# Four late pairs scored with queries on partitions and weights transposed by DMA, in clustered attention followed by a gated MLP, with a listed order of operations

## The chip, the cores and the metric

The kernel runs on one core of a Trainium2 chip. The metric is the device time of one launch in microseconds (us). Five engines work side by side, each with its own instruction queue in program order: TensorE (PE in the profile, PEld its weight loads), VectorE (DVE), ScalarE (ACT), GpSimd (POOL) and SyncE (SP). SP here does nothing but issue DMAs. PSUM holds what TensorE writes; SBUF holds everything else.

## The reference

```python
# q, k, v: (4, 8, 768, 64); centroids: (8, 16, 64)
q_assign = argmax(q_n . c_n)            # nearest of 16 centroids, per head
k_assign = argmax(k_n . c_n)
scores = where(q_assign == k_assign, q @ k.T / sqrt(64), -1e9)
scores = scores - max(scores, -1)
attn = exp(scores); attn = attn / (sum(attn, -1) + 1e-9)
x = (attn @ v), heads side by side      # (4, 768, 512)

h = maximum(x @ w_in, 0)                # w_in (512, 1024)
u, v = h[..., :512], h[..., 512:]
v_n = (v - mean(v)) / sqrt(var(v) + 1e-6)
v_s = w_spatial @ v_n + b_spatial       # over the 768 positions
out = (u * v_s) @ w_out                 # (4, 768, 512)
```

A query with no key in its cluster gets equal weights on all keys, since every score is -1e9 before the maximum is taken off.

## The kernel before

**Work.** There are 4 batches of 8 heads; the kernel takes the heads in 16 pairs, numbered 0 to 15, four to a batch. 768 positions are NT = 6 blocks of P = 128. To keep precision, each operand is split into a high and a low f16 part (`hq` and `lo` for keys and queries, `vhl` for values, `pt[:, 0]` and `pt[:, 1]` for the weights), and products are summed in PSUM.

**`prep(n)`** loads keys and queries of a pair, transposed (`raw`), and values (`vraw`), splits them, and works out the cluster of each key and query as one-hot rows. Those rows, scaled by PEN, stand below the 64 rows of the head in `hq`, so that a matmul over 80 rows adds a bonus where clusters agree. The low parts are made by `low`, on POOL for the entries of `POOL_LOWS` (a scaling and a subtraction, L531 and L532), and in one VectorE operation elsewhere (L533). `values` makes the parts of V and also the sums of V over all positions (for pairs 8 to 15 by a VectorE reduction `vs`, L684, and two small matmuls, L685), which go by two small DMAs into `mean`.

**`shifts(n)`** works out the largest score of every query ahead of attention. For each head it scores queries against keys with the high parts alone, with queries on partitions (L728: 6 matmuls of 512 columns and 6 of 256), reduces each group over the keys on VectorE (L735, nine per head, into `nm`), and turns the result into three columns on ScalarE (L752, L755). A DMA transpose (`sht`, L761) and a small copy (L762) put them as rows into `hq`.

**`attend(n)`** goes over the six key blocks k of each head with keys on partitions. `scores` does 4 matmuls into a PSUM buffer `sc` (L782, L784; the row of L784 takes the query's maximum off). ScalarE does the exponential into `p32` (L788) and rounds it into `pt[:, 0]` (L790), POOL makes `pt[:, 1]` (L791). With keys on partitions `pt` is already what the next matmul needs, and `values` (L796) adds 18 small matmuls into `av`. For k = 0 it also adds six matmuls of `hq` with `mean`, which serve the queries with no key in their cluster. The sum of weights is a 65th column. At the end of a head the result is divided, split again (L815 to L820) and, for the pair, transposed by one DMA into `xT` (L822).

**`mlp(b)`** runs the dense layers of batch b on TensorE in groups of matmuls of 512 columns (L840: `win` with `xT`, `wsp` with `vn`, `wou` with `gT`), which are put between the attention of the batch behind it. The product `u * v_s` is split on VectorE and POOL (L901 to L903) and transposed by DMA (`gT`, L904).

**Order.** Every operation is an object with an engine, a cost, what it comes after and the buffers that it takes. `Plan.run` goes through a modelled time with these costs, and at each step takes from what is ready on the engine that is free first the operation with the lowest due time plus key:

```python
k = o.key if o.key >= FILLER else (g if o.due is None else o.due) + o.key
if pick is None or (k, o.seq) < pick[:2]:
    pick = (k, o.seq, o)
```

The engines' queues follow this order. Buffers go round in rings: `r_sc` has 2 PSUM buffers of 768 columns in use, `r_acc` 4 of 512, `r_p32` 3, `r_pt` 4, `raw` and `vraw` 1 each, `hq` and `lo` 4. All DMAs but the stores of results stand on SP's queue in this order.

```python
r_sc = R(None, "sc", None, None, 2, free_order=True, tiles=[...])
r_acc = R(None, "acc", None, None, 4, free_order=True, tiles=[...])
```

## Time and profile before

| | |
|---|---|
| median of 3 runs (lowest to highest) | 680.63 us (679.72 to 682.48) |
| the profiled execution: time, span | 677.58 us, 675.8 us |
| TensorE busy, mean granted clock | 629.0 us, 0.995 |
| VectorE, ScalarE, POOL busy | 467.3, 433.5, 440.9 us |
| data moved by DMA | 70.49 MB, 104 GB/s |

Busy time is the time in which at least one instruction of the engine runs; matmuls overlap, so the busy times of groups of matmuls add up to more than TensorE's. A granted clock of 1.00 is TensorE's full speed. "Idle before, releaser" in a row is the time in which the engine stood still in front of the instruction and what it waited for. SPq is SP's queue of DMA issues: a row of it shows how long the issue held the queue, not when the data land. The pairs follow one another; the first four fill the time to about 150 us, then the dense layers of the batch behind run beside the next four, and from 592 us on only the dense layers of batch 3 are left.

### The profile page before, as it was taken

What the parts mean: (1) busy time and instruction counts of PE and PEld (TensorE: products, weight loads), DVE (VectorE), ACT (ScalarE), POOL (GpSimd) and SP (SyncE); (2) the same over time, 40 slices, a digit from 0 to 9 for tenths busy, and PEclk for the clock granted to TensorE, in tenths of its full rate; (3) what the DMA queues carried; (4) which work ended last, traced back from release to release, by engine and by line L of the source; (5) the groups of instructions that cost most, each with busy time, mean ns of one, the idle gap of its engine ahead of it and who ended that gap; (6) DMA issues with size and microseconds to landing.
All of it is one profiled execution on the core that took longest, in us unless ns stands there. A gap on an engine that the chain in (4) does not pass through costs nothing.

```text
span 675.8 us, 16854 instructions
## 1 busy us (share of the span) xinstructions
PE 629.0 (93%) x6821; PEld 378.0 (56%) x6821; DVE 467.3 (69%) x939; ACT 433.5 (64%) x685; POOL 440.9 (65%) x312
## 2 busy tenths in 40 slices
PE   2877898999999999999999999999999999989996
PEld 2455565766556655566465655566555655634442
DVE  5889999999899989285898857285795720215210
ACT  3586998998788946297586748387594837422011
POOL 6764798998786965376678747567486856703210
PEclk9988999999999999999999999999999999999999
DMA  5666667567728374374615346263300213130123
GB/s 171 177 166 126 169 171 169 94 166 175 175 66 207 64 138 127 84 167 111 147 26 130 60 91 139 45 144 84 80 14 14 52 29 82 38 85 1 31 63 93
DMA packets 106029, 70.49 MB, mean 104 GB/s; under 512 B 89640, under 2 KB 92768, under 8 KB 105952
## 3 DMA queue, kind: packets, MB, share of 16 engines
q1 hardware_dynamic: 102352, 63.13, 41.5%
q10 hardware_dynamic: 3600, 6.30, 2.5%
q8 instruction: 53, 0.87, 0.5%
q14 instruction: 24, 0.20, 0.1%
HBM read 27.63 MB, written 6.29 MB: 50 GB/s over the span
## 4 chain that ended last, share of the span: by engine, by line
PE 60%; DVE 17%; DMA 7%; ACT 7%; POOL 4%; issue 3%; SPq 1%; ACTq 0%; POOLq 0%; DVEq 0%
PE acc L840 35%; PE acc L796 9%; DVE nm L735 8%; PE sc L782 5%; PE sc L784 5%; PE acc L728 4%; ACT p L788 3%; ACT pt L790 2%; DMA vraw<-in_vp_dram 2%; DMA oht<-ohx 1%; DMA gT<-ghl 1%; POOL pt L791 1%; SPq L662 1%; POOL raw L531 1%; DVE vs L684 1%
## 5 line engine op out<-in xcount | busy, mean ns | idle before, releaser
L791 POOL TENSOR_TENSOR pt<-p,pt 128x768 f16<-128x768 f32 x192 | 322.5, 1698 | 83.8 <-ACT pt L790 44.6
L788 ACT ACTIVATE p<-sc,plog 128x768 f32<-128x768 f32 x192 | 169.2, 898 | 46.6 <-PE sc L784 43.5
L735 DVE TENSOR_REDUCE nm<-acc 128x1 f32<-128x512 f32 (+1 forms) x288 | 180.5, 678 | 13.0 <-PE acc L728 12.7
L790 ACT CAST pt<-p 128x768 f16<-128x768 f32 x192 | 155.6, 830 | 14.7 <-PE acc L796 12.9
L796 PEld LDWEIGHTS <-pt 128*128 128x128 f16 x3456 | 124.8, 98 | 22.8 <-POOL pt L791 4.0
L796 PE MATMUL acc<-vhl,pt 128*128 128x65 f16 (+1 forms) x3456 | 133.0, 194 | 3.0 <-POOL pt L791 2.8
L840 PE MATMUL acc<-win,xT 128*128 128x512 f16 x576 | 129.8, 379 | 0.0
L728 PE MATMUL acc<-hq 80*128 80x256 f16 (+1 forms) x384 | 95.6, 335 | 9.1 <-DVE nm L735 3.9
L782 PE MATMUL sc<-hq,lo 128*128 128x512 f16 (+1 forms) x384 | 94.8, 328 | 5.1 <-ACT p L788 4.7
L840 PE MATMUL acc<-vn,wsp 128*128 128x512 f16 x432 | 97.0, 379 | 0.8 <-DVE nm L735 0.8
L784 PE MATMUL sc<-hq 81*128 81x512 f16 (+1 forms) x384 | 94.9, 328 | 0.0
L840 PEld LDWEIGHTS <-xT 128*128 128x128 f16 x576 | 55.1, 98 | 62.5
L901 DVE SCALAR_TENSOR_TENSOR u<-acc,bsp,u 128x512 f32<-128x512 f32 x24 | 17.9, 746 | 90.9 <-PE acc L840 90.9
L903 POOL TENSOR_TENSOR ghl<-u,ghl 128x512 f16<-128x512 f32 x24 | 27.8, 1158 | 69.1 <-DVE ghl L902 65.2
L840 PEld LDWEIGHTS <-wsp 128*128 128x128 f16 x432 | 41.7, 98 | 49.6 <-issue 1.3
L840 PE MATMUL acc<-wou,gT 128*128 128x512 f16 x288 | 65.6, 379 | 3.8 <-DMA gT<-ghl 3.8
L911 ACT ACTIVATE o<-acc 128x512 f32<-128x512 f32 x24 | 14.3, 596 | 62.0 <-PE acc L840 43.3
L728 PEld LDWEIGHTS <-hq 80*128 80x128 f16 x384 | 34.2, 99 | 32.3 <-issue 12.5
L784 PEld LDWEIGHTS <-hq 81*128 81x128 f16 x384 | 37.6, 98 | 26.1 <-issue 1.0
L782 PEld LDWEIGHTS <-lo 128*128 128x128 f16 x384 | 34.2, 98 | 30.3 <-issue 14.4
L840 PEld LDWEIGHTS <-gT 128*128 128x128 f16 x288 | 27.4, 98 | 35.6 <-DMA gT<-ghl 4.8
L882 POOL TENSOR_TENSOR vn<-v,vn 128x512 f16<-128x512 f32 x24 | 30.0, 1268 | 17.3 <-DVE vn L881 17.3
(124 smaller groups left out, 652.1 us busy)
## 6 DMA issues: line engine op xcount, KB each, us to landing
raw<-in_kqT_dram SPq DMA_DIRECT2D x15, 768.0 KB
vraw<-in_vp_dram SPq DMA_DIRECT2D x16, 384.0 KB
out_dram<-o ACTq DMA_DIRECT2D x24, 256.0 KB
hq<-hq SPq DMA_DIRECT2D x15, 384.0 KB
vn<-in_w_in_dram SPq DMA_DIRECT2D x8, 512.0 KB
hq<-lo SPq DMA_DIRECT2D x15, 192.0 KB
lo<-hq SPq DMA_DIRECT2D x15, 192.0 KB
wraw<-in_wsT_dram SPq DMA_DIRECT2D x12, 192.0 KB
```

Source lines behind the costliest of these rows:

```text
L728: T.matmul(out=acc.t[:, c:c + cs.stop - cs.start], lhsT=hq.t[0:R_SH, 1, h, t * P:(t + 1) * P], rhs=hq.t[0:R_SH, 0, h, cs], start=c == 0, s ...
L735: V.tensor_reduce(out=nm.t[:, t, k:k + 1] if n == 1 else nm.t[:, t:t + n, k], in_=src, axis=AX.X, op=ALU.max, negate=True)
L782: T.matmul(out=sc.t[:, cs], lhsT=lo.t[:, h, ks], rhs=hq.t[:, 2, h, cs], start=True, stop=False)
L784: T.matmul(out=sc.t[:, cs], lhsT=hq.t[0:R_E, 0, h, ks], rhs=hq.t[0:R_E, 1, h, cs], start=False, stop=True)
L788: o = op("ACT", 0.9, lambda sc=sc, p32=p32: A.activation(out=p32.t, in_=sc.t[:, 0:S], func=AF.Exp, bias=plog, scale=SC_UNIT), after=[o, m_ ...
L790: o = op("ACT", 0.83, lambda pt=pt, p32=p32: A.copy(out=pt.t[:, 0, :], in_=p32.t), after=[o], use=[p32], new=[pt], key=K_HI)
L791: o = op("POOL", 1.65, lambda pt=pt, p32=p32: G_.tensor_tensor(out=pt.t[:, 1, :], in0=p32.t, in1=pt.t[:, 0, :], op=ALU.subtract), after=[o ...
L796: T.matmul(out=av.t[:, t * (D + 1):t * (D + 1) + w], lhsT=lhsT, rhs=rhs, skip_group_check=True, **f)
L840: T.matmul(out=acc.t, lhsT=lr[m][0], rhs=lr[m][1], start=(m == 0), stop=(m == n - 1))
L882: l = op("POOL", 1.25, lambda t=t, v=v: G_.tensor_tensor(out=vn[:, 1, t, :], in0=v.t, in1=vn[:, 0, t, :], op=ALU.subtract), after=[h], use ...
L901: o = op("DVE", 0.75, lambda: V.scalar_tensor_tensor(out=u32.t, in0=acc.t, scalar=bsp[:, t:t + 1], in1=u32.t, op0=ALU.add, op1=ALU.mult), ...
L903: l = op("POOL", 1.156, lambda: G_.tensor_tensor(out=ghl.t[:, 1, :], in0=u32.t, in1=ghl.t[:, 0, :], op=ALU.subtract), after=[h], use=[u32, ...
```

## The change

Three things change in what is computed, and the order of all operations with them.

1. Pairs 9, 11, 13 and 15 (`ROWS`) have no `shifts` and no `mean`. They are attended by a new function, `attend_rows`, which goes over the six query blocks t with queries on partitions. The scores are the same four matmuls with the operands exchanged. VectorE finds each query's maximum from the scores themselves (one reduction over 768 keys and two operations on one column), and the exponential takes it as bias and a scale, which is 0 where no key is in the cluster. The weights now have queries on partitions, so a DMA transpose on SP (`ptT`, two buffers) turns the 128x1536 high and low weights of a block before 18 value matmuls.
2. `low` on POOL gives its scaling to ScalarE, and head 1 of pair 0 is no longer in `POOL_LOWS`.
3. The planner is gone. `Plan.run` takes the operations from a list of numbers, `ORDER`. A buffer taken "in order of freeing" is now the one whose last user has the earliest place in the list. The units of work become half pairs (`Unit`); `SPLIT` is False, so that the halves are the heads as before. In the function for results, the scale `f` is a name of its own. `vs` lies in a buffer for weights.

```diff
-POOL_LOWS = {(0, 1), (0, 2), (1, 0), (1, 1), (1, 2)}
+PTT_BUFS = 2
+ROWS = (9, 11, 13, 15)
+POOL_LOWS = {(0, 2), (1, 0), (1, 1), (1, 2)}
...
     def run(self):
...
+        for turn, i in enumerate(ORDER):
+            o = self.ops[i]
+            assert all(a.turn < turn for a in o.after)
+            for tok in o.new:
+                tok.ring.taken.append(tok)
+                tok.alloc()
+            o.turn = turn
+            if o.fn is not None:
+                o.fn()
+
+ORDER = [
+    0, 10, 7, 9, 1, 12, 2, 11, 3, 13, 4, 162, 14, 15, 16, 17, 18, 19, 20, 21, 163, 22, 6, 23,
...
         if (n, x) in POOL_LOWS:
-            o = op("POOL", 1.0, lambda: G_.tensor_scalar(out=raw(), in0=raw(), scalar1=scale, scalar2=None, op0=ALU.mult), after=after, use=use, key=key)
+            o = op("ACT", lambda: A.activation(out=raw(), in_=raw(), func=AF.Copy, scale=scale), after=after, use=use)
...
     def values(...):
...
+        if n in ROWS:
+            X["v"] = [o_vh, o_vl]
+            return
...
     def shifts(...):
+        if u.n in ROWS:
+            return
...
+    def attend_rows(u):
+        n, h = u.n, u.part
+        X = pair[n]
+        hq, lo, vh = X["hq"], X["lo"], X["vhl"]
+        av = r_acc.new()
+        prev = None
+        for t in range(NT):
+            sc, p32, pt, ptT, nq = r_sc.new(), r_p32.new(), r_pt.new(), r_ptT.new(), r_nq.new()
+            ts = slice(t * P, (t + 1) * P)
+
+            def scores(sc=sc, ts=ts):
+                for cs in halves:
+                    T.matmul(out=sc.t[:, cs], lhsT=hq.t[:, 2, h, ts], rhs=lo.t[:, h, cs], start=True, stop=False)
+                for cs in halves:
+                    T.matmul(out=sc.t[:, cs], lhsT=hq.t[0:R_SH, 1, h, ts], rhs=hq.t[0:R_SH, 0, h, cs], start=False, stop=True)
+
+            o = last["sc"] = op("PE", scores, after=X["go"][h] + [last.get("sc")] + exps[-2:-1], use=[hq, lo], new=[sc])
+            o = op("DVE", lambda sc=sc, nq=nq: V.tensor_reduce(out=nq.t[:, 0:1], in_=sc.t[:, 0:S], axis=AX.X, op=ALU.max, negate=True), after=[o], use=[sc], new=[nq])
+            o = op("DVE", lambda nq=nq: V.tensor_scalar(out=nq.t[:, 1:2], in0=nq.t[:, 0:1], scalar1=LIM, scalar2=SC_UNIT, op0=ALU.is_lt, op1=ALU.mult), after=[o], use=[nq])
+            o = op("DVE", lambda nq=nq: V.tensor_scalar(out=nq.t[:, 2:3], in0=nq.t[:, 0:1], scalar1=nq.t[:, 1:2], scalar2=P_LOG * LN2, op0=ALU.mult, op1=ALU.add), after=[o], use=[nq])
+            o = op("ACT", lambda sc=sc, p32=p32, nq=nq: A.activation(out=p32.t, in_=sc.t[:, 0:S], func=AF.Exp, bias=nq.t[:, 2:3], scale=nq.t[:, 1:2]), after=[o], use=[sc, nq], new=[p32])
+            exps.append(o)
+            o = op("ACT", lambda pt=pt, p32=p32: A.copy(out=pt.t[:, 0, :], in_=p32.t), after=[o], use=[p32], new=[pt])
+            o = op("POOL", lambda pt=pt, p32=p32: G_.tensor_tensor(out=pt.t[:, 1, :], in0=p32.t, in1=pt.t[:, 0, :], op=ALU.subtract), after=[o], use=[p32, pt])
+            o = sp(lambda pt=pt, ptT=ptT: nc.sync.dma_start_transpose(ptT.t, pt.t.rearrange("p a s -> p (a s)")), after=[o], use=[pt], new=[ptT])
+
+            def values(ptT=ptT, t=t):
+                def mm(w, lhsT, rhs, **f):
+                    T.matmul(out=av.t[:, t * (D + 1):t * (D + 1) + w], lhsT=lhsT, rhs=rhs, skip_group_check=True, **f)
+
+                for k in range(NT):
+                    mm(D + 1, ptT.t[:, k], vh.t[:, k, h, 0:D + 1], start=t == 0 and k == 0, stop=False)
+                    mm(D, ptT.t[:, k], vh.t[:, k, h, D + 2:], start=False, stop=False)
+                    mm(D + 1, ptT.t[:, NT + k], vh.t[:, k, h, 0:D + 1], start=False, stop=t == NT - 1 and k == NT - 1)
+
+            prev = op("PE", values, after=[o, prev] + X["v"], use=[ptT, vh] + ([av] if t else []), new=[] if t else [av])
+        results(u, av, prev)
```

How the list moves instructions is shown at three places. The first is POOL at the start of the program. Before, behind the last constants, it makes the low parts of head 1 of pair 0, of its values (`vhl_89`), of both heads of pair 1 and of its values (`vhl_90`):

```order
L531 TENSOR_SCALAR raw<-raw 128x768
L532 TENSOR_TENSOR lo<-raw,hq 128x768
L531 TENSOR_SCALAR vraw<-vraw 128x768
L532 TENSOR_TENSOR vhl_89<-vraw,vhl_89 128x12x64
L531 TENSOR_SCALAR raw<-raw 128x768
L532 TENSOR_TENSOR lo<-raw,hq 128x768
```

After, there is no scaling, the values of pair 0 come first, and a constant stands behind the lows; then the first pass over weights (`pt`) follows:

```order
L523 TENSOR_TENSOR vhl_89<-vraw,vhl_89 128x12x64
L523 TENSOR_TENSOR lo<-raw,hq 128x768 x2
L409 MEMSET ohx 128x768
L409 MEMSET ohx 128x6x2
L523 TENSOR_TENSOR vhl_90<-vraw,vhl_90 128x12x64
L838 TENSOR_TENSOR pt<-p_512,pt 128x768
```

The five scalings have left POOL, and one subtraction with them.

The second place is ScalarE up to the first exponential. Before, the high parts of pair 1 (L611) stand there, and then the columns of pair 0:

```order
L611 ACTIVATE hq<-raw 128x768 x2
L591 CAST hq<-sc_111 16x768
L752 ACTIVATE shx_86<-nl 128x6
L755 ACTIVATE shx_86<-nl,flag 128x6 x2
L759 CAST hq<-sc_111 19x768
L668 ACTIVATE vhl_90<-vraw 128x12x64
L474 ACTIVATE win<-acc_113 128x512
L788 ACTIVATE p_404<-sc_110,plog 128x768
```

After, the scalings (L522) are here, and a second pair of high parts (L597), that of pair 2, comes ahead of the first exponential (L833):

```order
L597 ACTIVATE hq<-raw 128x768 x2
L522 ACTIVATE raw<-raw 128x768 x2
L580 CAST hq<-sc_113 16x768
L746 ACTIVATE shx_86<-nl,flag 128x6 x2
L743 ACTIVATE shx_86<-nl 128x6
L597 ACTIVATE hq<-raw 128x768 x2
L684 ACTIVATE wl_95<-w_281 2x2x65
L654 ACTIVATE vhl_90<-vraw 128x12x64
L522 ACTIVATE vraw<-vraw 128x768
L751 CAST hq<-sc_112 19x768
L453 ACTIVATE win<-acc_117 128x512
L833 ACTIVATE p_502<-sc_113,plog 128x768
```

Pair 2's preparation moved to before pair 0's first scores; on TensorE, too, the matmuls for the clusters of pairs 1 and 2 now stand ahead of them.

The third place is SP from pair 15's second shift to the end of the last attention. Before, its queue has the second shift of pair 15 (`sht`) and then transposes of results (`xT`) and of gated products (`gT`) only:

```order
L761 DMA_TRANSPOSE sht<-shx_86 128x6x128
L762 DMA hq<-sht 3x768
L904 DMA_TRANSPOSE gT<-ghl 128x8x128
L822 DMA_TRANSPOSE xT_106<-xhl 128x12x128
L904 DMA_TRANSPOSE gT<-ghl 128x8x128 x4
L822 DMA_TRANSPOSE xT_106<-xhl 128x12x128
L904 DMA_TRANSPOSE gT<-ghl 128x8x128 x6
```

After, the last of pair 14's copies are followed by the transposes of pair 15's weights, between which the others stand:

```order
L788 DMA_TRANSPOSE ptT<-pt 128x12x128 x3
L973 DMA_TRANSPOSE gT<-ghl 128x8x128
L788 DMA_TRANSPOSE ptT<-pt 128x12x128 x5
L891 DMA_TRANSPOSE xT_106<-xhl 128x12x128
L788 DMA_TRANSPOSE ptT<-pt 128x12x128 x4
L973 DMA_TRANSPOSE gT<-ghl 128x8x128
L891 DMA_TRANSPOSE xT_106<-xhl 128x12x128
L973 DMA_TRANSPOSE gT<-ghl 128x8x128 x10
```

The twelve transposes of pair 15 are new in this queue; its two shifts are gone, and ten transposes of products instead of six follow the last transpose of results.

More of the change, by code (lines that the diff above doesn't have):

```diff
@@ L125 @@
 class Op:
[L126 to L139 removed]
+    __slots__ = ("eng", "fn", "after", "new", "turn")
 class Plan:
@@ L186, in run @@
-        free = {"PE": 0.6, "ACT": 1.1, "DVE": 0.63, "POOL": 0.57, "SP": 0.5, "NONE": 0.0}
-        wait = {e: [] for e in LAG}
-        hw = [0.0, 0.0]
-        port = 0.0
-        lanes = []
-        columns = {}
-        def arm(o):
-            o.ready = max([o.at] + [a.end + lag(a, o.eng) for a in o.after] + [a.s for a in o.order])
-            wait[o.eng].append(o)
-        def gate(o):
-            t = o.ready
-            for tok in o.new:
-                r = tok.ring
-                if r.free_order and r.tiles is not None:
-                    first = min(r.free_at(i, o.eng) for i in range(r.bufs))
-                    if first == float("inf"):
-                        return None
-                    t = max(t, first)
-                elif r.free_order and len(r.taken) >= r.bufs:
-                    old = r.taken[-r.bufs].users
-                    if any(u.end is None for u in old):
-                        return None
-                    t = max([t] + [u.end + lag(u, o.eng) for u in old])
-            return t
@@ L434 @@
+    o = op("POOL", lambda: G_.tensor_tensor(out=nrm, in0=ss, in1=half, op=ALU.pow), after=[o, m_half])
     o = chain("DVE", [
[L435 to L438 removed]
@@ L765, in attend, with top, scores, most @@
-    def attend(n):
+        nm = r_nm.new()
+        if n:
+            sx, sht = r_shx.new(), r_sht.new()
+        else:
+            sx = X["sx"]
+        tops = []
+        needs = X["rows"][0] if u.split else X["rows"][u.part]
+        def top(parts, cols):
+            acc = r_acc.new()
+            m = len(parts)
+            def scores():
+                for i, (j, cs) in enumerate(parts):
+                    h, t = u.blocks[j]
+                    w = cs.stop - cs.start
+                    T.matmul(out=acc.t[:, i * w:(i + 1) * w], lhsT=hq.t[0:R_SH, 1, h, t * P:(t + 1) * P], rhs=hq.t[0:R_SH, 0, h, cs], start=i == 0, stop=i == m - 1, skip_group_check=True)
+            o = op("PE", scores, after=needs, use=[hq], new=[acc])
+            def most():
+                src = acc.t if m == 1 else acc.t.rearrange("p (t c) -> p t c", t=2)
+                V.tensor_reduce(out=cols(nm.t), in_=src, axis=AX.X, op=ALU.max, negate=True)
+            tops.append(op("DVE", most, after=[o], use=[acc] + ([nm] if tops else []), new=[] if tops else [nm]))
@@ new lines, in shifts, with col @@
+        for j in range(HT):
+            j0, j1 = (j, j + HT) if u.split else (2 * j, 2 * j + 1)
+            for i in (j0, j1):
+                top([(i, halves[0])], lambda x, i=i: x[:, i, 0:1])
+            top([(j0, halves[1]), (j1, halves[1])], lambda x, j0=j0, j1=j1: x[:, j0:j1 + 1:j1 - j0, 1])
+        nl = r_nl.new()
+        o = op("DVE", lambda: V.tensor_reduce(out=nl.t, in_=nm.t, axis=AX.X, op=ALU.min), after=tops + [m_half], use=[nm], new=[nl])
+        def col(c):
+            return sx.t[:, :, R_SH + c] if n else oh0[:, :, 2 + u.part, 1, c]
@@ new lines, in shifts @@
+        first = {"new": [sx], "use": [nl]} if n else {"use": [nl, sx]}
+        cols = [op("ACT", lambda: A.activation(out=col(0), in_=nl.t, func=AF.Copy, scale=1.0 / PEN), after=[o, c_sh], **first)]
+        for c in range(2):
+            m = 2.0 ** (-MEAN_LOG * c)
+            cols.append(op("ACT", lambda c=c, m=m: A.activation(out=col(1 + c), in_=nl.t, func=AF.Relu, bias=flag[:, c:c + 1], scale=2 * m / LIM), after=[o, c_sh, m_half], use=[nl, sx]))
+        if n == 0:
+            tp = r_sc.new()
+            h = u.part
+            tr = op("PE", lambda: [T.matmul(out=tp.t[0:2 * C, t * P:(t + 1) * P], lhsT=oh0[:, t, 2 + h].rearrange("p e c -> p (e c)"), rhs=id16, start=True, stop=True) for t in range(NT)], after=cols, use=[sx], new=[tp])
+            u.shift = op("ACT", lambda: A.copy(out=hq.t[R_OH:R_END, 1, h, :], in_=tp.t[0:R_END - R_OH, 0:S]), after=[tr], use=[hq, tp])
+            return
@@ L821, in attend @@
-        war = xread.get(b - 2, [])
-        xd = sp(lambda: nc.sync.dma_start_transpose(xTs[b % 2][:, p].rearrange("p j a q -> p (j a) q"), xhl.t.rearrange("p j a q -> p (j a q)")), 1.25, after=xls + war, use=[xhl], turn=True, key=K_XD)
-        xdone.setdefault(b, []).append(xd)
+        av = r_acc.new()
+        prev = None
+        if u.split:
+            chunks = [(h, slice(u.part * HT * P, (u.part + 1) * HT * P), 512 * h) for h in range(2)]
+            go = X["go"][0]
+        else:
+            chunks = [(u.part, cs, cs.start) for cs in halves]
+            go = X["go"][u.part]
```

641 lines of the change are left out of this document (257 added, 384 removed), and 131 rows, old and new, of the table ORDER.

## The prediction

> **What bounds the kernel now.** I read the page first, then the busy time by stage, then the rows of single operations. From the page, the span and the engines' busy time:
>
> ```profile
> span 675.8 us, 16854 instructions
> PE 629.0 (93%) x6821; PEld 378.0 (56%) x6821; DVE 467.3 (69%) x939; ACT 433.5 (64%) x685; POOL 440.9 (65%) x312
> ```
>
> The profiled execution took 677.58 us, 1.78 around its span; the runs' median is 680.63, which is 0.45% more. I make the sum against the span and scale at the end.
>
> Busy time in four stretches (columns: length, then busy us and instructions of PE, weight loads, DVE, ACT, POOL, the granted clock, DMA share, GB/s). The first is the start, up to 592 are the sixteen pairs with the dense layers of batches 0 to 2 beside them, and behind 592 the layers of batch 3 stand alone:
>
> ```profile
> 0.00:102.00 102.00, 75.82 (x990) 50.90 (x991) 89.77 (x209) 73.51 (x116) 71.26 (x60) 0.97 0.64 163
> 102.00:265.00 163.00, 153.94 (x2004) 100.11 (x2002) 152.75 (x288) 135.36 (x223) 131.24 (x85) 1.00 0.60 142
> 265.00:592.00 327.00, 322.90 (x3481) 192.90 (x3480) 204.99 (x393) 212.07 (x328) 221.50 (x154) 1.00 0.36 80
> 592.00:676.00 84.00, 76.33 (x353) 34.06 (x350) 19.81 (x51) 12.54 (x21) 16.88 (x16) 1.00 0.23 55
> ```
>
> From 265 to 592, where pairs 8 to 15 are attended, TensorE is idle for 4.1 of 327 us, and no other engine passes 68%. So a matmul taken away there is time taken away, as long as nothing new makes TensorE wait. Up to 265 it is idle for 26.2 + 9.1 = 35.3 us, with VectorE at 88 and 94%: there the other engines set the pace. All four changed pairs (9, 11, 13, 15) lie in the third stretch.
>
> **What the change removes from TensorE.** A matmul's own duration holds its drain, so I price by the distance to the next start. From the timeline of TensorE:
>
> ```profile
> 449.36 0.81 PE L728 MATMUL acc<-hq 80*128 80x512 f16 x4
> 450.00 0.49 PE L782 MATMUL sc<-hq,lo 128*128 128x512 f16 x2
> ...
> 450.66 0.34 PE L796 MATMUL acc<-mean,hq 83*128 83x65 f16 x6
> 450.84 0.72 PE L796 MATMUL acc<-vhl,pt 128*128 128x65 f16 x18
> 451.40 0.81 PE L728 MATMUL acc<-hq 80*128 80x512 f16 x4
> ...
> 458.45 0.38 PE L685 MATMUL acc<-vs,one 128*2 128x128 f32 x2
> 458.76 0.50 PE L782 MATMUL sc<-hq,lo 128*128 128x512 f16 x2
> ```
>
> Four of the pass for the maxima (L728) take 0.64; a head has twelve, so 1.92, and eight heads 15.4. Six matmuls of the mean take 0.18; eight heads, 1.4. The sums of a pair (L685) take 0.31; four pairs 1.2, and with the short waits around them I take 1.8. Together 18.6 us. The scores (four matmuls, 0.65) and the value passes (18, 0.56) keep their number and size, with operands exchanged, so they cost nothing new. Nothing hid these 18.6 us: they lay on the full engine.
>
> **What it adds to the other engines.** From the page's groups:
>
> ```profile
> L791 POOL TENSOR_TENSOR pt<-p,pt 128x768 f16<-128x768 f32 x192 | 322.5, 1698 | 83.8 <-ACT pt L790 44.6
> L788 ACT ACTIVATE p<-sc,plog 128x768 f32<-128x768 f32 x192 | 169.2, 898 | 46.6 <-PE sc L784 43.5
> L735 DVE TENSOR_REDUCE nm<-acc 128x1 f32<-128x512 f32 (+1 forms) x288 | 180.5, 678 | 13.0 <-PE acc L728 12.7
> L790 ACT CAST pt<-p 128x768 f16<-128x768 f32 x192 | 155.6, 830 | 14.7 <-PE acc L796 12.9
> ```
>
> Per head VectorE loses nine reductions over 512 columns and gets six over 768. One over 768 takes between 0.68 and 1.02 (all of it fixed, or all by columns); I take 0.95, nearer the columns. Behind each stand two one-column operations on SBUF. Rows of their likes (min/median/max ns):
>
> ```profile
> L873 DVE TENSOR_SCALAR a<-mv x12: 153/170/1597, 169.0 to 622.7; 128x2 f32<-128x2 f32 x12
> L815 DVE TENSOR_SCALAR rc<-acc x32: 141/152/166, 58.7 to 590.3; 128x6 f32<-128x6 f32 x32
> ```
>
> L815 reads PSUM and never takes over 0.17; L873 has both ends in SBUF, as the new ones do, and now and then takes 1.6, about one POOL pass (1.698). I take 0.4 for each. So VectorE goes from 9 x 0.68 = 6.1 to 6 x (0.95 + 0.8) = 10.5 a head, 35 us more over eight heads, on 205 of 327: still under 80%, so it costs nothing as throughput. As latency it puts 1.75 between scores and exponential in each tile, so that each of the two score buffers is held for 0.2 + 1.75 + 0.9 = 2.85 instead of 1.1. Counted in matmuls, the new order leaves 2.5 us at the shortest place and mostly 4 to 8 between a score pass and the next but one; I cost this at nothing.
>
> The Trainium skill speaks against the change here: GPSIMD Engine Reference, section "8. Key points", says that GpSimd shares its SBUF interfaces with VectorE and contends with VectorE's instructions in a two-port mode or with two SBUF inputs. The two rows above agree that such waits happen, with a median of 170 ns as the usual case; by the rule at its worst the sum would be that of the second rival below, by the rows it stays as I take it.
>
> ScalarE loses three small columns a head; POOL's pass per tile stays.
>
> **The transposes.** 48 new DMA transposes of 128x1536 f16 stand on SP's queue, ordered with its loads, and lie between POOL's pass and the value matmuls. xT is the same size; sht is half, gT two thirds. From the chain, from SP's timeline, and from the DMA answer for 500 to 506 us, in which sht is nearly alone (share of 16 engines last):
>
> ```profile
> 108.43 5.86 DMA xT<-xhl
> ...
> 500.90 1.21 SPq L761 DMA_TRANSPOSE sht<-shx  x1
> 503.65 0.76 SPq L762 DMA_DIRECT2D hq<-sht  x1
> ...
> q1 hardware_dynamic: 806, 0.20, 17.1%
> ```
>
> Half size lands in 2.75 on a quiet queue, of which 17.1% of 6 us, 1.03, moves data. Full size: 2.75 + 1.03 = 3.8, the low end. In a crowded stretch xT took 5.86, the high end. From the tail, gT beside a store of results:
>
> ```profile
> 662.28 5.34 PE L840 MATMUL acc<-wou,gT 128*128 128x512 f16 x24
> 665.11 1.23 SPq L904 DMA_TRANSPOSE gT<-ghl  x1
> 669.36 2.76 PE L840 MATMUL acc<-wou,gT 128*128 128x512 f16 x12 [1.74 <-DMA gT<-ghl]
> ```
>
> That is 4.25 with some company, which I take, since the third stretch has a DMA share of 0.36 only. The 48 add 48 x 2.06 = 99 us of data time, a share of 0.32 in some 308 us, so the queues stand near 0.7, not full. SP itself was held 1.21 us by sht; at once to twice that, 48 take 58 to 116 of the 308 us, and eight shift transposes with their copies (1.21 + 0.76 each) go, so SP has room too.
>
> ptT has two buffers, so a transpose waits for the value pass two tiles earlier: two tiles need 4.25 + 0.2 drain + 0.56 = 5.0 us. Counting the matmuls that the new order puts between the first and the last value pass of each changed pair (twelve matmuls of 512 columns are 2.6 us; scores and value passes as above), I get 44, 34, 41 and 30 us for pairs 9, 11, 13 and 15, eleven steps each, so 5.5 to 8 us for two tiles. On average that covers 5.0; the tightest single places hold 4.4 + 0.56. In the second half of pair 15, for example, 12 dense matmuls, a score pass, a value pass and 12 dense ones stand between the value passes of tiles 0 and 2 (6.4 us), but 12, a value pass and 6 between those of tiles 1 and 3 (4.4). Pair 15 has 30 us where 27.5 are needed, the least cover. At 5.86 two tiles need 6.6, eleven steps 36.4, and pairs 11 and 15 lose 2 + 6 = 8 us. So the transposes cost between 0 and 8; I take 2.5, nearer the quiet row. Between a tile's scores and its values the order leaves 10 to 25 us of matmuls; the whole chain (0.2 + 0.95 + 0.8 + 0.9 + 0.83 + 1.7 + 4.25) needs 9.6, so it is covered, but by little in the last half pair. SP's loads for the next pair now stand behind transposes that wait for POOL; a pair lasts 327/8 = 41 us, in which a load may come a few us later, and that hides it.
>
> **The start.** The lows of pairs 0 and 1 leave POOL in part: five scalings go (four to ScalarE, one with its subtraction to VectorE).
>
> ```profile
> 2.12 4.96 DMA raw<-in_kqT_dram
> ...
> L531 POOL TENSOR_SCALAR raw<-raw 128x768 f32<-128x768 f32 x3 | 6.4, 2132 | 7.5 <-ACT hq L545 4.2 <-DVE nm L735 3.3
> ...
> 11.95 0.21 PE L562 MATMUL acc<-cmh,lo 128*128 128x32 f16 x1 [3.74 <-POOL lo L532]
> ...
> 29.85 0.90 ACT L788 ACTIVATE p<-sc,plog 128x768 f32<-128x768 f32 x1 [2.05 <-PE sc L784]
> ```
>
> 5 x 2.13 + 1.64 = 12.3 us leave POOL ahead of its first pass, and TensorE's wait of 3.74 for the second head goes. But the new order puts the preparation of pair 2 ahead of the first scores, so the first exponential may come no earlier than 29.85. Bounds: a gain of 12 (POOL's 12.3 in full), a loss of 5 (one more load in front of the scores: a load of raw took 4.96 at the start). The rest of the listed order up to 265 moves too, against 35.3 idle us. I take a gain of 4.
>
> **The tail.** The last value group now has 18 matmuls (3.9 us) between the last spatial group and itself, where 24 (5.3) stood before the wait of 1.74: 1 us more (between 0 and 1.4).
>
> **Sum.** 675.8 - 18.6 - 4 + 2.5 + 1 = 656.7; + 1.78 = 658.5; times 680.63/677.58, 661.5.
>
> **Rivals.**
> *The transposes set the pace (slower).* If they land in 7.5 us on average, behind 768 KB loads on the same queue, two tiles need 8.3 and eleven steps 45.4: the four pairs lose 1 + 11 + 5 + 15 = 32. 675.8 - 18.6 - 4 + 1 + 32 = 686.2, so 691. It decides from about 7, where the loss eats the gain. For it: all share one queue. Against: the longest in the chain is 5.86, in a busier stretch. Chance 6%.
>
> *The saving turns into waits on the score buffers (no change).* If both small operations wait for POOL as long as L873's longest (1.6), the hold is 0.2 + 0.95 + 3.2 + 0.9 = 5.25; thirteen places of the new order are shorter than that, by 17 us together, and 661.5 + 17 = 679. That decides where it happens in nearly every tile. For it: POOL passes of 1.7 fill half of each tile's time. Against: L873's median of 170 ns, beside POOL at 68%. This is the contention of which the Trainium skill speaks in GPSIMD Engine Reference, "8. Key points". Chance 7%.
>
> *The clock falls in the new waits.* From the busy times of the start and its timeline:
>
> ```profile
> 53.00:57.00 4.00, 2.45 (x9) 0.76 (x8) 4.00 (x9) 3.43 (x7) 2.43 (x2) 1.00 0.29 66
> 57.00:61.00 4.00, 3.77 (x66) 3.58 (x66) 4.00 (x9) 1.83 (x5) 0.85 (x1) 0.57 0.22 49
> 57.91 3.75 PE L796 MATMUL acc<-vhl,pt 128*128 128x65 f16 x74
> ```
>
> After 4 us at 61% busy the clock was 0.57, and 74 value matmuls took 3.75 instead of 74 x 0.031 = 2.3. Once in each of eight halves costs 8 x 1.5 = 12: 674. The Trainium skill has the rule (TensorE: Matmul & The Clock Gate, "What's actually happening": half rate after an idle window of about 3.4 us); here the trace agrees, and the waits I expect are of 1 us between full stretches. Chance 6%.
>
> *The listed order packs the start far better.* Half of the 35.3 idle us gone, 17.6 instead of 4: 648. For it: every engine is below 95% up to 265. Against: VectorE's 242 us of work by then stay. Chance 19%.
>
> **How the numbers follow.** My forecast has 60%, with 653 to 669 as its own range; 2% is left for a loss I don't see. The range 648 to 673 leaves out the slower and the unchanged case and the far ends. Faster by over 0.5%, about what a measurement can tell, is 60 + 6 + 19 = 85%, within it 7, slower 6 + 2 = 8.
>
> **What would show it.** Right: TensorE still over 96% busy while pairs 8 to 15 run, that stretch some 16 to 19 us shorter, ptT landing in 3.8 to 5, waits of value matmuls for it of a few us in all and mostly in pairs 11 and 15, the small VectorE operations at 0.2 to 0.5. Wrong: ptT over 6.5 us, score matmuls waiting long for exponentials, a clock below 1 after 265, or a first exponential behind 33 us.

## The result and the profile after

The changed kernel takes 650.22 us (median of 4 runs, 649.68 to 650.55), beside 680.17 us (678.21 to 682.48) for the kernel before: a ratio of 0.956, 95% interval 0.953 to 0.959. The forecast was 661.5 with a range of 648 to 673, so the sign held, and the range by 2 us: the saving of 30 us was 11 larger than forecast. The profiled execution took 650.09 us, 1.8 around its span. One of the four runs of the version with the maxima put back (below) took 1064 us at a granted clock of 0.67, and is left out of its times.

The page after, span and busy time, in the same columns as before:

```profile
span 648.3 us, 16703 instructions
PE 612.3 (94%) x6669; PEld 367.1 (57%) x6669; DVE 463.8 (72%) x992; ACT 436.3 (67%) x661; POOL 429.4 (66%) x306
```

TensorE has 152 matmuls fewer (96 of the maxima, 48 of the means, 8 of the sums) and is busy 16.7 us less. Its idle time went from 46.8 to 36.0 us. So of 27.5 us of span, 16.7 are busy time that went and 10.8 are waits that went; the forecast had 1 us of the second kind.

Busy time by stretch; the last attention now ends near 557 us instead of 592, so the third stretch ends at 563:

```profile
0.00:102.00 102.00, 80.83 (x992) 52.09 (x993) 95.02 (x215) 73.86 (x118) 58.47 (x52) 0.85 0.58 152
102.00:265.00 163.00, 156.23 (x2161) 105.30 (x2159) 148.45 (x299) 147.97 (x238) 139.27 (x91) 1.00 0.63 142
265.00:563.00 298.00, 295.40 (x3152) 173.86 (x3151) 198.15 (x426) 201.04 (x284) 212.11 (x146) 1.00 0.78 147
563.00:649.00 86.00, 79.83 (x370) 35.84 (x367) 22.16 (x55) 13.42 (x23) 19.52 (x18) 0.99 0.25 62
```

TensorE's idle time is the length less the first number: 21.2, 6.8, 2.6 and 6.2 us (0.7 of the last lie behind the span), where before it was 26.2, 9.1, 4.1 and 7.7 (0.2 behind). TensorE is busy for 99% of the stretch with the four changed pairs. The DMA share there went from 0.36 to 0.78: the transposes.

TensorE's waits from 265 us on, total, times and longest; first the kernel before, then the one after:

```profile
PE acc L840 <- DMA gT<-ghl: 3.8, 2, 2.1
PE acc L685 <- DVE nm L735: 1.3, 1, 1.3
PE acc L685 <- DVE vs L684: 1.0, 1, 1.0
PE acc L728 <- DVE nm L735: 1.0, 2, 0.7
PE acc L728 <- DVE w L694: 0.3, 1, 0.3
PE acc L840 <- DVE nm L735: 0.3, 1, 0.3
```

```profile
PE acc L792 <- DMA ptT<-pt: 2.2, 5, 0.6
PE acc L909 <- DMA gT<-ghl: 1.8, 1, 1.8
```

The waits of the other five rows (3.9 us) are gone, and so is one of the two waits for gT. By the timeline 2.3 us of the 3.9 stood at the sums of pairs 11 and 13 and 1.0 at the maxima of pair 15, all of which the change removes; the rest stood beside maxima and sums. The transposes brought 2.2 us of new ones, 1.7 of them in pairs 11 and 15. The start went another way than forecast; ScalarE's first exponential, then the engines from 20 to 61 us:

```profile
35.35 0.90 ACT L833 ACTIVATE p<-sc,plog 128x768 f32<-128x768 f32 x1
```

```profile
20.00:41.00 21.00, 15.11 (x120) 7.79 (x119) 20.93 (x43) 10.75 (x19) 4.22 (x3) 0.50 0.52 152
41.00:61.00 20.00, 19.77 (x207) 12.03 (x206) 17.25 (x32) 14.80 (x25) 11.87 (x8) 0.76 0.48 125
```

It comes at 35.35 instead of 29.85. POOL is nearly empty from 20 to 41 us, VectorE full, and TensorE's clock stands at half. Still, by 265 us the new order has run 992 + 2161 = 3153 matmuls where the old one had run 2994. Weighing the matmuls of each shape by their spacing at full clock (0.216 us for 512 columns, 0.109 for 256, 0.031 for 64 or 65, and so on) gives an estimate of how far TensorE's work has come: the new order is 0.6 us ahead at 150 us, 3.3 at 220 and some 5 at 265.

The new operations, rows of the tile nq (min/median/max ns), the transposes on SP, and their landings where the chain of waits passes through them (start, us):

```profile
L781 DVE TENSOR_REDUCE nq<-sc x48: 923/957/959, 301.7 to 544.8; 128x1 f32<-128x768 f32 x48
L782 DVE TENSOR_SCALAR nq<-nq x48: 122/153/155, 303.9 to 545.8; 128x1 f32<-128x1 f32 x48
L783 DVE TENSOR_SCALAR nq<-nq x48: 173/214/215, 306.4 to 546.0; 128x1 f32<-128x1 f32 x48
L784 ACT ACTIVATE p<-sc,nq x48: 968/991/1012, 306.7 to 546.3; 128x768 f32<-128x768 f32 x48
```

```profile
L788 SPq DMA_TRANSPOSE ptT<-pt x48: 1287/1470/2510, 311.0 to 550.3; - x48
```

```profile
335.98 3.81 DMA ptT<-pt
...
535.77 4.93 DMA ptT<-pt
```

### The profile page after: what moved, and what is told of

The parts are those of the page before. It is cut to its first block, busy times and chain, and to the rows that moved or that the text cites. A ratio compares the mean times of both kernels' runs of the same rounds, so it can differ in the third digit from the quotient of the medians.

```text
span 648.3 us, 16703 instructions
## 1 busy us (share of the span) xinstructions
PE 612.3 (94%) x6669; PEld 367.1 (57%) x6669; DVE 463.8 (72%) x992; ACT 436.3 (67%) x661; POOL 429.4 (66%) x306
## 4 chain that ended last, share of the span: by engine, by line
PE 64%; DVE 16%; DMA 8%; ACT 5%; issue 4%; POOL 1%; SPq 1%; POOLq 0%; DVEq 0%; ACTq 0%
PE acc L909 34%; PE acc L843 8%; DVE nm L726 6%; PE acc L720 5%; PE sc L823 4%; PE sc L825 4%; DMA ptT<-pt 4%; PE acc L792 2%; PE sc L776 2%; PE sc L778 2%; ACT p L833 2%; DVE lo L524 2%; ACT pt L837 1%; DMA gT<-ghl 1%; DVE nq L781 1%
## 5 line engine op out<-in xcount | busy, mean ns | idle before, releaser
L726 DVE TENSOR_REDUCE nm<-acc 128x1 f32<-128x512 f32 (+1 forms) x216 | 140.7, 681 | 29.7 <-PE acc L720 29.0
L833 ACT ACTIVATE p<-sc,plog 128x768 f32<-128x768 f32 x144 | 128.2, 901 | 18.2 <-PE sc L825 14.1
L837 ACT CAST pt<-p 128x768 f16<-128x768 f32 x144 | 117.6, 831 | 3.9 <-DMA ptT<-pt 1.8
L843 PEld LDWEIGHTS <-pt 128*128 128x128 f16 x2592 | 92.5, 97 | 16.8 <-issue 2.8
L843 PE MATMUL acc<-vhl,pt 128*128 128x65 f16 (+1 forms) x2592 | 98.4, 193 | 1.9 <-POOL pt L838 1.7
L720 PE MATMUL acc<-hq 80*128 80x512 f16 (+1 forms) x288 | 79.8, 348 | 10.0 <-DVE nm L726 6.1
L823 PE MATMUL sc<-hq,lo 128*128 128x512 f16 (+1 forms) x288 | 72.3, 333 | 2.6 <-ACT p L833 2.5
L825 PE MATMUL sc<-hq 81*128 81x512 f16 (+1 forms) x288 | 72.2, 332 | 0.0
L784 ACT ACTIVATE p<-sc,nq 128x768 f32<-128x768 f32 x48 | 47.4, 990 | 34.2 <-DVE nq L783 18.6
L781 DVE TENSOR_REDUCE nq<-sc 128x1 f32<-128x768 f32 x48 | 45.5, 952 | 32.9 <-PE sc L778 31.0
```

What stands on the lines that cost most here:

```text
L720: T.matmul(out=acc.t[:, i * w:(i + 1) * w], lhsT=hq.t[0:R_SH, 1, h, t * P:(t + 1) * P], rhs=hq.t[0:R_SH, 0, h, cs], start=i == 0, stop=i = ...
L726: V.tensor_reduce(out=cols(nm.t), in_=src, axis=AX.X, op=ALU.max, negate=True)
L781: o = op("DVE", lambda sc=sc, nq=nq: V.tensor_reduce(out=nq.t[:, 0:1], in_=sc.t[:, 0:S], axis=AX.X, op=ALU.max, negate=True), after=[o], u ...
L784: o = op("ACT", lambda sc=sc, p32=p32, nq=nq: A.activation(out=p32.t, in_=sc.t[:, 0:S], func=AF.Exp, bias=nq.t[:, 2:3], scale=nq.t[:, 1:2] ...
L823: T.matmul(out=sc.t[:, c:c + cs.stop - cs.start], lhsT=lo.t[:, h, ks], rhs=hq.t[:, 2, h, cs], start=True, stop=False)
L825: T.matmul(out=sc.t[:, c:c + cs.stop - cs.start], lhsT=hq.t[0:R_E, 0, h, ks], rhs=hq.t[0:R_E, 1, h, cs], start=False, stop=True)
```

## The experiments

Theory: the change saves the TensorE work that it takes away, the transposes cost a few us, and the rest comes from waits that the new order takes away. Rivals: the row scoring saves more than its matmuls; or the start alone holds the rest.

Times below are medians. The kernel before ran beside each of them and took 673.6 to 683.1 us in single runs. The changed kernel's own four runs lie within 0.9 us, and versions of it are set against its 650.22. It did not run again beside them. The medians of the kernel before were 676.7 to 677.9 us there and 680.2 beside the result, so a difference of up to some 3 us between versions is not shown by the times alone.

**The removed work put back.**

```diff
                 for cs in halves:
+                    T.matmul(out=sc.t[:, cs], lhsT=hq.t[0:R_SH, 1, h, ts], rhs=hq.t[0:R_SH, 0, h, cs], start=True, stop=True)
+                for cs in halves:
                     T.matmul(out=sc.t[:, cs], lhsT=hq.t[:, 2, h, ts], rhs=lo.t[:, h, cs], start=True, stop=False)
```

> The changed kernel, with TensorE's removed pass for the maxima put back as work that nobody needs: each of the 48 row tiles first runs two more matmuls (80 rows, 512 + 256 columns) into its score buffer and then overwrites them. Nothing else is added: no reduction, no wait. Theory A (TensorE is the bound in this stretch, so each of its microseconds is a microsecond of the kernel): 48 x 0.32 = 15.4 us more, 665.6 (663 to 668). Theory B (the saving came mostly from waits and from VectorE's passes that went with the maxima, TensorE has room): at most 5 us more, 650 to 655.

Measured: 661.6, 661.8 and 664.6 us, ratio to before 0.978 (0.973 to 0.983). That is 11.6 us more by the middle one and 14.5 by the profiled one, whose span is 662.8. That is far above theory B and 1 us below theory A's range of 663 to 668: some three quarters or more of the added TensorE time became time of the kernel. Theory A holds in the main. Windows with the third stretch 16 us longer:

```profile
265.00:579.00 314.00, 313.19 (x3263) 184.95 (x3262) 199.26 (x431) 201.86 (x287) 211.07 (x147) 1.00 0.73 140
```

TensorE is idle there for 0.8 us where the changed kernel has 2.6: a part of the added work filled waits. So the removed matmuls were worth close to what their spacing said, a little less.

**No transposes.**

```diff
-            o = sp(lambda pt=pt, ptT=ptT: nc.sync.dma_start_transpose(ptT.t, pt.t.rearrange("p a s -> p (a s)")), after=[o], use=[pt], new=[ptT])
+            o = sp(None, after=[o])
...
-                    mm(D + 1, ptT.t[:, k], vh.t[:, k, h, 0:D + 1], start=t == 0 and k == 0, stop=False)
+                    mm(D + 1, pt.t[:, 0, k * P:(k + 1) * P], vh.t[:, k, h, 0:D + 1], start=t == 0 and k == 0, stop=False)
```

> The changed kernel without its 48 DMA transposes: the value matmuls of the four pairs read the untransposed weights, in five buffers of pt and none of ptT. This leaves out the transposition, so the four pairs' result is not attention; all other instructions and the listed order stay. Theory A (the order covers the transposes, they cost nothing): 650 (648.5 to 651). The prediction's term (2.5 us of uncovered waits): 647.7. If the 8 us that TensorE's rows show as waits for ptT are all on the path: 642.

Measured: 646.84 us (646.76 to 647.07), 3.4 less. The prediction's term was 2.5. The third stretch:

```profile
265.00:563.00 298.00, 297.76 (x3169) 176.20 (x3168) 198.35 (x428) 200.97 (x284) 214.10 (x147) 1.00 0.38 84
```

Idle time falls from 2.6 to 0.2 us, 17 more matmuls have run by the end of the stretch (some 3.7 us at the spacing of the dense layers), and the DMA share falls from 0.78 to 0.38. So the trace bears the 3.4 us out. Of the 8 us in which weight loads and matmuls are shown waiting for ptT, most lay beside matmuls still running.

**Row scoring in the old order.** The kernel before as a list, with row scoring put in by hand; the dependences and buffers are those of the changed kernel, and all scalings stay on POOL.

```diff
-ORDER = [ ...the new list ]
+ORDER = [ ...the old order; in pairs 9, 11, 13, 15: exponentials, casts and POOL passes 8 places later, transposes 8 behind POOL, values 32 later ]
```

> The kernel before, its order of operations written out as a list, with the row scoring of the four pairs put in place: their passes for maxima, means and sums left out, each exponential some 1.7 us and each value pass some 6 us later in the list, the reductions and transposes in between; everything else, the start too, stands as before. Theory A (the row scoring gives its 18.6 us of TensorE work, the rest of the 30 comes from the new order): 680.2 - 18.6 plus 0 to 8 for a roughly placed order, 662 to 670. Theory B (the row scoring alone gives all 30, since waits went with the passes): 650 to 655.

Measured: 756.84 us (756.08 to 758.24), 11% slower than before. Both theories missed. TensorE's waits from 265 us on:

```profile
PE acc L792 <- DMA ptT<-pt: 26.6, 16, 3.8
PE sc L776 <- ACT p L784: 15.8, 13, 2.7
```

My placing was no fair order, but it shows that the cover is made by the order, not by the engines' room: but for the scalings these are the changed kernel's instructions, with 42 us in these two waits alone.

**The planner with the change in it.** Here the planner places everything: it has durations for the new steps, its old constants, and for the new steps keys of old ones.

```diff
-POOL_LOWS = {(0, 1), (0, 2), (1, 0), (1, 1), (1, 2)}
+ROWS, POOL_LOWS = (9, 11, 13, 15), {(0, 2), (1, 0), (1, 1), (1, 2)}
...
+                o = sp(lambda pt=pt, ptT=ptT: nc.sync.dma_start_transpose(ptT.t, pt.t.rearrange("p a s -> p (a s)")), 1.25, after=[o], use=[pt], new=[ptT], turn=True, key=K_HI)
```

> The kernel before with its planner and the planner's constants, and with the row scoring of the four pairs and the moved scalings in it; the planner chooses the order. Theory S (what the change takes from TensorE is saved under any order that a planner with durations makes): 680 - 18.3 + 3.4 = 665, 660 to 672. Theory T (the row scoring pays only in an order made for it, as the two roughly placed lists suggest): 680 or more.

Measured: 724.2 us (722.6 to 728.3), ratio to before 1.072 (1.067 to 1.077). Theory T. Its page, two of TensorE's waits behind 265 us, and the third stretch:

```profile
PE 643.6 (89%) x6669; PEld 379.4 (52%) x6669; DVE 466.5 (64%) x992; ACT 439.2 (60%) x661; POOL 429.8 (59%) x306
...
PE acc L875 <- DMA ptT<-pt: 17.5, 15, 4.4
PE acc L901 <- DMA xT<-xhl: 5.1, 1, 5.1
...
265.00:563.00 298.00, 271.30 (x2755) 157.86 (x2753) 181.97 (x390) 183.49 (x262) 182.38 (x124) 0.93 0.61 120
```

These are the changed kernel's 6669 matmuls. They are busy for 31.3 us more (643.6 against 612.3) at a granted clock of 0.939 against 0.976, and the span of 726.5 leaves 82.9 us idle against 36.0. The windows above show TensorE at full clock (1.00), at half (0.50) or at a mix of both. So mean clocks of 0.939 and 0.976 are some 89 and 31 us at half clock (twice the shortfall, times the span, an estimate), and 58 us more at half pace cost up to 29 us, about the 31.3. In the planner's order the row scoring is a loss of 46 us against the kernel before beside it (677.75), in waits and in slow matmuls around them. That a planner with its constants set anew for the new steps would lose too is not shown. (The scalings are on ScalarE in it, as in the changed kernel; by a run below that is worth 2 us at most, and to the good.)

**The new order without row scoring.** ROWS empty, the list kept, the shifts of pairs 8 to 15 placed by me.

```diff
-ROWS = (9, 11, 13, 15)
+ROWS = ()
...
+ORDER = [ ...the new list without the row steps; shifts of pairs 8 to 15 spread over the half pair ahead ]
```

> The changed kernel with the four pairs scored as before (keys on partitions, maxima, means and sums again), in the new listed order; the shifts of pairs 8 to 15 are set evenly into the half pair ahead of the one that needs them, the other operations stand where the list has them. Theory A (the new order is worth some 11 us by itself): 650.2 + 18.6 = 669 and 0 to 8 more for the rough placing, 669 to 677, below the 680 of before. Theory B (the order is worth nothing): 680 or more.

Measured: 825.07 us (820.6 to 831.4). By the number this is theory B, but it tells nothing on the order's worth, since my placing brought new waits. The largest, 52 of the some 147 us lost:

```profile
PE sc L826 <- DMA hq<-sht: 51.9, 16, 7.4
```

Scores wait for shift rows at the start of each half; the buffers for shifts are single, and a spread that ends with the half before leaves no time for the transpose. What the new order would be worth to the old scoring stays open.

**Splicing the starts.** Old start, new rest; new start, old rest; the cut at 150 us, where both orders have run 55 or 56 exponentials, and at 220 us.

```diff
+ORDER = [ ...the first 900 operations of the old order, then the others as the new list has them ]
```

> The changed kernel with the start of the one before: the first 900 operations (some 150 us, with all five scalings on POOL and the low of pair 0's second head there too) in the old order, all that is left in the new list's order. The sets of operations behind and ahead of the cut differ by 38. Theory P (the prediction's term, the start is worth 4 us): 654. Theory Q (the traces: by 150 us 56 exponentials have run in the one and 55 in the other, so this start is worth nothing): 649 to 652. Theory R (all of the 11 us beyond the forecast come from the start): 661.

> The other half of the same question: the kernel before, all pairs scored with keys on partitions, with the changed kernel's first 908 operations (some 150 us, lows with scalings on ScalarE) and then its own order. Theory P: 676. Theory Q: 678 to 681. Theory R: 669.

> As the run before it, with the changed kernel's first 1343 operations (some 220 us, into pair 6 or 7) ahead of the old order. No row scoring, no transposes. Theory P (4 us by 265 us): 676. Theory Q (the traces: TensorE's idle time up to 265 us fell from 35.3 to 27.9 us, some 3 of it filled by matmuls at half clock, most of it behind 150 us): 673 to 677. Theory R: 669.

Measured: 661.04 (656.98 to 664.05), 679.55 (677.81 to 681.14) and 679.38 us (678.30 to 681.60); the kernel before took 677.0 beside them, so the two with new starts are 0.3 to 0.4% slower than it (ratios 1.004 and 1.003). The first fits theory R, the second theory Q, the third none. The rows of the first behind its cut, and SP's rows of the changed kernel:

```profile
160.69 1.01 PE L720 MATMUL acc<-hq 80*128 80x512 f16 x2 [6.25 <-DMA hq<-oht]
...
150.00:200.00 50.00, 42.81 (x529) 26.75 (x528) 38.80 (x79) 34.45 (x56) 32.97 (x22) 0.90 0.46 104
```

```profile
136.96 1.64 SPq L648 DMA_DIRECT2D hq<-oht  x2
...
139.10 1.38 SPq L648 DMA_DIRECT2D hq<-oht  x2
```

These are the one-hot rows of pair 6. The new list copies them ahead of 141 us; in the old start they were issued at 154.79, as its last steps, and the new rest asks for them at once, at 154.4. The 6.25 us of waiting and the clock of 0.90 stand at the seam. In work weighed by spacing this run is 11 us behind the changed kernel at 220 us, most of the 14.0 by which its span is longer. The seams of the other two cost as well: the second run is 0.6 us ahead of the old order at 150 us and 2 behind it at 220; the third is 3.3 ahead at 220, where its cut is, and 1 behind at 265. So the splices do not measure what the parts of the order are worth. The traces of the two whole kernels do: 0.6 us of work up to 150, some 5 up to 265 (TensorE is busy for 49.33 us from 150 to 200 in the changed kernel and for 48.45 in the one before). That the gain comes from having the next pair ready earlier fits these rows and is not shown by itself.

**Scaling on POOL, and the lows of pair 2.**

```diff
-            o = op("ACT", lambda: A.activation(out=raw(), in_=raw(), func=AF.Copy, scale=scale), after=after, use=use)
+            o = op("POOL", lambda: G_.tensor_scalar(out=raw(), in0=raw(), scalar1=scale, scalar2=None, op0=ALU.mult), after=after, use=use)
```

> The changed kernel with the four scalings of pairs 0 and 1 on POOL again, at the place in the list where they stand on ScalarE. POOL is idle for 44 of the first 102 us, VectorE for 7: theory Q (VectorE sets the pace at the start, POOL has room): 650 to 653. If POOL's first passes set the pace: 4 x (2.1 - 0.83) = 5 us more, 655.

```diff
-POOL_LOWS = {(0, 2), (1, 0), (1, 1), (1, 2)}
+POOL_LOWS = {(0, 2), (1, 0), (1, 1), (1, 2), (2, 0), (2, 1), (2, 2)}
...
+ORDER = [ ...the new list, with three more scalings on ScalarE ]
```

> The changed kernel with the three lows of pair 2 done as those of pair 1, scaling on ScalarE and subtraction on POOL, instead of one operation on VectorE each. VectorE is busy for 95.0 of the first 102 us, POOL for 58.5, ScalarE for 73.9. Theory Q (VectorE sets the pace of the start): up to 3 x 0.95 = 2.9 us less, 647 to 649.5. If the start is set by the loads or by the chain through TensorE: 650. If ScalarE's three scalings of 0.83 stand ahead of the first exponentials: up to 2.5 more, 652.7.

Measured: 652.14 us (651.30 to 652.69) with the scalings on POOL, 1.9 more; 648.80 (648.00 to 649.35) with the lows of pair 2 off VectorE, 1.4 less. Both are inside theory Q's bounds, and both below the 0.5% that can be told safely: neither's runs overlap with the changed kernel's, but those did not run beside them. VectorE's share of the first 102 us with the second:

```profile
0.00:102.00 102.00, 80.31 (x1024) 52.53 (x1025) 92.66 (x214) 77.46 (x123) 63.03 (x56) 0.87 0.62 157
```

It falls by 2.4 us, and 32 matmuls more are run by then: VectorE does bear on the start's pace; that any of it reaches the end is not shown.

**Twice the reduction.**

```diff
-lambda sc=sc, nq=nq: V.tensor_reduce(out=nq.t[:, 0:1], in_=sc.t[:, 0:S], axis=AX.X, op=ALU.max, negate=True)
+lambda sc=sc, nq=nq: [V.tensor_reduce(out=nq.t[:, 0:1], in_=sc.t[:, 0:S], axis=AX.X, op=ALU.max, negate=True) for _ in range(2)]
```

> The changed kernel, each of the 48 reductions over a row tile's scores done twice: 0.95 us more between scores and exponential in each tile, 46 us more on VectorE in all, TensorE's work as it is. The prediction's term (the score buffers are held longer at no cost; VectorE has room, since it is busy for 198 of 298 us there): 650 to 653. If the hold of the score buffers or VectorE were near the limit already: 0.95 us a tile, up to 46, 660 and more.

Measured: 667.58 us (666.35 to 674.20), 17.4 more, 0.36 a tile. TensorE's largest wait, and the third stretch:

```profile
PE sc L776 <- ACT p L784: 10.0, 10, 1.9
...
265.00:563.00 298.00, 282.33 (x3010) 166.46 (x3009) 237.72 (x466) 198.35 (x281) 205.58 (x141) 0.99 0.73 139
```

Ten score passes of the four pairs now wait for exponentials, which in the changed kernel these passes do not (0.1 us idle ahead of them in all). VectorE is at 80%. So there is cover, but it does not hold 0.95 us more in every tile; how much of the loss is the held buffers and how much VectorE's fuller queue is not told apart.

**More cover in the tail.** On top of the lows of pair 2, six matmuls of value tile 3 behind the last spatial group.

```diff
 ORDER = [
 ...
-    p3 (6), s5 (18), p3 (6), p4 (12), p5 (12)
+    s5 (18), p3 (6), p3 (6), p4 (12), p5 (12)
```

> The kernel of the run with the lows of pair 2 on POOL, and in the last dense layers six matmuls of value tile 3 stand behind the last spatial group instead of ahead of it, so that 24 matmuls lie between that group and the wait for gT, as in the kernel before, where 18 do in the changed one. Theory U (the prediction's tail term turned round: more cover, less wait): 1.0 to 1.3 us less, 647.5 to 647.8. Theory V (the last transpose cannot start before the 12 matmuls of tile 3 have read the buffer that it needs, 2.8 us behind the spatial group, and lands 3.0 us later as in the changed kernel or 4.25 as in the one before): 0 to 1.1 us less, 647.7 to 648.8, with a wait of 0.6 to 1.8 left.

Measured: 649.12 us (647.93 to 650.22), no gain over 648.80: theory V's end without a gain. The last groups on TensorE, first of the changed kernel, then of this one:

```profile
632.13 4.05 PE L909 MATMUL acc<-vn,wsp 128*128 128x512 f16 x18
636.02 4.05 PE L909 MATMUL acc<-wou,gT 128*128 128x512 f16 x18
641.89 2.76 PE L909 MATMUL acc<-wou,gT 128*128 128x512 f16 x12 [1.83 <-DMA gT<-ghl]
```

```profile
631.01 4.05 PE L909 MATMUL acc<-vn,wsp 128*128 128x512 f16 x18
634.89 5.34 PE L909 MATMUL acc<-wou,gT 128*128 128x512 f16 x24
642.03 2.76 PE L909 MATMUL acc<-wou,gT 128*128 128x512 f16 x12 [1.79 <-DMA gT<-ghl]
```

With 18 or with 24 matmuls ahead of it the wait is 1.8 us. The last transpose of the changed kernel in the chain of waits (start, us), and SP's row of the new run, whose last number but the count is the start of the last one:

```profile
638.82 3.03 DMA gT<-ghl
```

```profile
L973 SPq DMA_TRANSPOSE gT<-ghl x4: 1232/1232/2183, 619.6 to 637.7; - x4
```

It starts 2.6 us behind the spatial group in both (632.13 + 4.05 = 636.2 to 638.8, and 635.1 to 637.7), when POOL's last pass ends (638.80 and 637.67), so theory V's reason, the buffer, is not what held it. But TensorE goes on 3.1 us later with 18 and 4.3 with 24 (642.03). Why it lands later is not shown. One thing differs: the store of a result was issued 0.7 us ahead of this transpose in the changed kernel (638.14), and 0.6 behind it in the new run (638.31), as in the kernel before (665.70, behind 665.11), where the landing took 4.25.

## Why the prediction was right, and where it was short

**Right: what bounds the kernel, and the removed work.** The term of the sum was 18.6 us, 0.6 of it waits. The trace has 16.7 us less busy time, with some matmuls of the start at half clock, and 18.3 us less work by the spacing of each shape; putting the maxima back cost 11.6 to 14.5 of 15.4. TensorE is the bound there. The third stretch became 29 us shorter and not 16 to 19, since some 5 us of work was done ahead of it and 17 more dense matmuls (3.7 us) are left behind its end.

**Right: the transposes.** 2.5 forecast, 3.4 measured. They land in 3.8 to 4.9 us where the chain passes them (4.25 taken), SP was held 48 x 1.47 = 71 us (58 to 116 forecast), and the DMA share of the third stretch is 0.78 (0.7). They move data for 0.40 x 298 / 48 = 2.5 us each, against 2.06.

**Right, but with less room than I thought: VectorE.** The chain between scores and exponential is 0.957 + 0.153 + 0.214 = 1.3 us instead of 1.75, since the small operations never waited for POOL (0.155 and 0.215 at most, against 0.4 each). On the rule of the Trainium skill that I weighed (GPSIMD Engine Reference, section "8. Key points"), no run here shows that contention in these operations. At 1.3 us the hold costs nothing, as forecast; at 2.3 it costs 0.36 a tile, so "mostly 4 to 8 us of cover" was too generous a reading of the order. The row that I took as their like, L873, works on two columns, and its longest ends with a POOL pass (at 515.31 and 515.28 us); its counterpart in the changed kernel still takes up to 0.85. The 96 one-column operations never did. Why is not shown.

**About right in size, wrong in its way: the start.** Forecast a gain of 4. TensorE's idle time up to 265 us fell by 5.0 + 2.3 = 7.3, of which some 2 are matmuls running at half clock: by the spacing of each shape some 5 us more work was done by then. But the first exponential came 5.5 us later, behind the 33 us that I had named as a sign of failure, POOL's freed time stayed empty, and only 0.6 us of the work was gained in the first 150 us. Four of the five scalings that leave POOL, the cause that I priced, cost 1.9 when put back, less than the times can show. So the size came out by luck.

**Mis-sized: the waits behind 265 us.** I forecast +2.5 for transposes, +1 for the tail and -0.6 for the waits around the sums, 2.9 in all; measured is 8.8 - 0.7 of idle time against 11.8 - 0.2 before, -3.5. Two terms failed:
- *The waits that go with the removed passes.* I priced those beside one sum and took 0.6; five rows of the wait view, which stood in the trace of before, hold 3.9 us, 3.3 of it at sums and maxima that the change removes.
- *The tail.* I counted the matmuls that cover the last wait, 18 against 24. The last run shows that this number does not set the wait: with 24 the last transpose takes 1.2 us longer to reach TensorE, about what the six matmuls cover (1.3), and the wait stays at 1.8. The other wait for gT, 2.1 us, went as well, so the tail's waits gained 2 instead of losing 1.

**Mis-sized: the scale.** The profiled execution of before was 0.45% below the median of its three runs, and I carried that over to the sum, +3.0 us. The changed kernel's profiled execution is at its median (650.09 and 650.22). It was the three runs that lay high: beside the other versions the medians of the kernel before were 676.7 to 677.9, and the profiled execution took 677.58.

By busy and idle time these add up: in the span 656.7 was forecast and 648.3 measured, 8.4 less, made of 3.3 more up to 265 us, 6.4 more behind it and 1.3 less of removed work; 3.0 of scale make the 11.3 us.

**The rivals.** That the transposes set the pace or that waits lower the clock did not happen in this order (the 0.99 of the last stretch comes from behind 647 us), but did in two others: the planner's order of the same instructions ran at a clock of 0.939 with 17.5 us of waits for ptT. The Trainium skill's rule (TensorE: Matmul & The Clock Gate, "What's actually happening": half rate after an idle window of about 3.4 us) agrees in kind only. In the planner's run TensorE was busy for 1.6 of the 3.4 us ahead of a stretch at half clock (468.5 to 471.9 us), and in the kernel before for 2.2 of the 3.4 us ahead of the slow stretch that I cited (53.9 to 57.3), so the window need not be empty. The rival of a far better start named 648, close to the 650 measured, but its mechanism did not come: the start gave some 5 of its 17.6 us, and the nearness is chance.

So I was right on the order given and wrong to treat it as a bystander: I priced the list as a gain at the start, while in the two other orders tried the row scoring lost, 724 and 757 against 650.

**Open.** How the saving divides between list and row scoring, since each alone was tried only in orders that are bad for it; what the new order would be worth to the old scoring; and what a planner set anew for the row scoring would make.

The lowest median of a version that does the whole attention is 648.8 us, with the lows of pair 2 on ScalarE and POOL; 0.2% below the changed kernel is less than the times can show.

## What to carry to other kernels

Where one engine is full, price removed work by its spacing, and then read all waits of that engine in the stretch: those that hang on the removed steps go too (3.3 us here). A change that swaps an engine's work for a longer chain (reduction, exponential, transpose) is worth what the order covers: look at the order for it, and don't expect the saving from a scheduler tuned for the old chain. Cover is not only the count of instructions ahead of a wait; in the last run here the transfer took longer when more stood ahead.

## What the runs showed of the hardware that I had not expected

The same 6669 matmuls were busy for 612.3 us in one order and 643.6 in another, at mean granted clocks of 0.976 and 0.939. In the second order, from 265 us on, a wait of 1.6 to 5.1 us stands at each stretch of half clock; behind one of 4.39 us for ptT, 18 value matmuls took 1.17 us instead of 0.72. So, as far as the traces show, waits cost some 31 us of slow matmuls beside 47 us more of idle time.

The clock at the start of a trace can mislead. In the run with the new start up to 220 us it reads 1.00 from 20 to 41 us, in the changed kernel 0.50, but in both the first score passes follow one another by 0.64 us for two matmuls, where 0.33 is the pace at full clock. The spacing is the safer measure.

The kernel before scattered between 673.6 and 683.1 us over all its runs; the four runs of the changed kernel lay between 649.7 and 650.6 and those without transposes between 646.8 and 647.1. The new list alone is not the reason, since with two reductions it took 666.4 to 674.2. 48 transposes of 128 x 1536 elements took the DMA share of their stretch from 0.38 to 0.78, and cost 3.4 us.
